# Transposing the third batch's x by DMA instead of on TensorE: pairs 8, 9 and 10 of a block-sparse attention kernel that feeds a mixture of experts

## The chip, the cores and the metric

One core of a Trainium2 chip (trn2); the rounds of the experiments ran on three such chips, each beside the kernel before. The metric is the device time of one execution in microseconds (us); most executions of a kernel agree within 0.3%.

Engine names: PE is TensorE, PEld its weight loads, DVE VectorE, ACT ScalarE, POOL GpSimd, SP SyncE. The suffix q (SPq) means the engine's instruction queue. L508 is line 508 of the kernel's file.

## The reference

Two parts. Attention over q, k, v of shape (4, 8, 768, 64): every query sees the keys less than 16 positions away and 24 block summaries of the whole sequence (maximum of k, mean of v over 32 positions). Its output, laid out as x of shape (3072, 512), feeds a mixture of 8 experts with a Sinkhorn-normalized gate:

```python
logits = x @ w_gate                      # (3072, 8)
P = np.exp(logits - logits.max())
for _ in range(8):                       # 8 rounds over ALL rows
    P /= P.sum(1, keepdims=True) + 1e-9
    P /= P.sum(0, keepdims=True) + 1e-9
    P *= N / E
for e in range(8):
    out += P[:, e:e+1] * (np.maximum(x @ w1[e], 0) @ w2[e])
```

The Sinkhorn rounds need the logits of all four batches, so they cannot start before the last batch's x is complete.

## The kernel before

Attention works in "pairs": pair i holds two heads, pairs 0 to 3 are batch 0, 4 to 7 batch 1, 8 to 11 batch 2, 12 to 15 batch 3. Each pair's normalized output `xs` must be transposed into `xT`, which expert 0, the gate's logits and all other experts read. There are two ways, both already in the kernel:

```python
def to_xT(i, h=None):                    # way 1: PE transposes into PSUM ...
    t = at.pop(("xs", i, h or 0))
    tx = at["tx", i, h] = bank("a", "tx", BF16)
    for g in range(G if h is None else HG):
        nc.tensor.transpose(tx[:, g * 128:(g + 1) * 128],
                            t[:, g, :, :].rearrange("p j d -> p (j d)"), ident)

def x_out(eng, i, h=None):               # ... and a copy by ACT or DVE into xT
    ...
    copy(eng, xT[:, i % PB, t0:t0 + n], at.pop(("tx", i, h))[:, 0:n])

def x_dma(i):                            # way 2: one DMA transpose, SBUF to SBUF
    t, t0 = at.pop(("xs", i, 0)), i // PB * S
    nc.sync.dma_start_transpose(
        out=xT[:, i % PB, t0:t0 + S].rearrange("c (g t) -> c g t", g=G),
        in_=t[:].rearrange("p g j d -> p (g j d)"))
```

The order of the instructions on every engine is static. While the kernel is built, a small planner simulates the engines with assumed durations and lists each unit where it would run. This is the planner's choice of the two ways (`lag` is time until landing):

```python
X_BY_DMA = 12
# ... at the end of pair_whole(i, prio), PB = 4:
if i >= X_BY_DMA and i % PB < PB - 1:
    U["xt", i] = add("SP", 1.5, lambda: x_dma(i), [U["no", i, 0], U["no", i, 1]], prio)
    U["x", i] = add("DMA", 1.7, None, [U["xt", i]], prio, lag=2.0)
    return
buf = Buffer("a")
U["xt", i] = add("PE", 0.35, lambda: to_xT(i), [U["no", i, 0], U["no", i, 1]], prio, opens=[buf])
U["x", i] = add({"ACT": 0.8, "DVE": 0.55}, 0, lambda: x_out(U["x", i].on, i), [U["xt", i]], prio, uses=[buf])
```

So before the change pairs 12, 13 and 14 go by DMA and all others, also the last pair of each batch, by PE. Expert 0's matmuls serve as filler for PE between attention's units. The last piece is how expert 1's weights are fetched. POOL issues two loads of 1 MB, and first reads a column of the last pair's transposed k and q, so that the loads wait for those transposes:

```python
def transposed():
    r = (NP - 1) % NB                    # NP - 1 is pair 15
    nc.gpsimd.tensor_copy(out=warm[:, 0:1], in_=kT[r][0:32, 0:1])
    nc.gpsimd.tensor_copy(out=warm[:, 1:2], in_=qT[r][0:32, W:W + 1])
    ...                                  # two more, of the near values
last[0] = add("POOL", 0.3, transposed, ...)
load("w1n", lambda: load_w1(1), 0.85, 5.0)
load("w2n", lambda: load_w2(1), 0.85, 5.0)
```

The softmax here doesn't subtract the row's maximum and nothing guards it: scores larger than these inputs give would overflow.

Of the kernel before, what the change touches and what calls it, by code (L numbers as in the profile page):

```python
# [32 lines left out]
class Plan:  # L33
# [7 lines left out]
    def add(self, eng, cost, fn, deps=(), prio=0.0, opens=(), uses=(), lag=0.0):  # L41
        u = Unit(eng, cost, fn, [d for d in deps if d is not None], prio, list(opens), lag)
        for b in list(opens) + list(uses):
            b.users.append(u)
        if uses and eng != "PE":
            u.prio -= 100.0
        self.units.append(u)
        return u
# [64 lines left out]
def kernel(  # L113
# [28 lines left out]
    VD = D + 1  # L142
    NEH = 3
    BY_DMA = 12
    X_BY_DMA = 12
    WHOLE = 12

    const = ctx.enter_context(tc.tile_pool(name="const", bufs=1))
# [71 lines left out]
    with tc.tile_pool(name="attn", bufs=1) as attn, \  # L220
# [295 lines left out]
        def x_dma(i):  # L516
# [4 lines that stand above are left out]
# [188 lines left out]
        def pair_whole(i, prio):  # L709
# [27 lines left out]
            for h in range(2):  # L737
# [5 lines left out]
                                    [U["A", i, h], U.get(("x", i - 2))], prio, uses=[buf])  # L743
            if i >= X_BY_DMA and i % PB < PB - 1:
                U["xt", i] = add("SP", 1.5, lambda: x_dma(i), [U["no", i, 0], U["no", i, 1]], prio)
# [175 lines left out]
```

## Time and profile before

| | before |
|---|---|
| time, median of 4 runs | 738.88 us (738.64 to 739.21) |
| span of the profiled execution | 740.0 us |
| PE transposes of x / DMA transposes of x | 78 / 3 |
| wait of PE at the last logits | 0.85 us |

The profiled execution itself took 741.82 us; PE's clock was halved in it from 14.2 to 21.0 us, before anything that the change touches.

The page's first part gives busy time, share of the span and number of instructions of each engine:

```profile
PE 730.5 (99%) x4300; PEld 355.8 (48%) x4300; DVE 369.2 (50%) x728; ACT 198.4 (27%) x339; POOL 95.8 (13%) x122
```

PE is busy 99% of the span. The stretch table (columns: stretch, its length, then busy time and count of PE, PEld, DVE, ACT, POOL; then PE's granted clock, 1.00 being full speed, DMA share, GB/s):

```profile
66.00:94.20 28.20, 27.36 (x314) 18.00 (x315) 26.89 (x74) 20.54 (x35) 15.68 (x22) 1.00 1.61 134
94.20:124.90 30.70, 30.50 (x293) 18.12 (x291) 20.11 (x55) 19.24 (x37) 6.48 (x14) 1.00 0.58 91
124.90:126.00 1.10, 0.25 (x7) 0.16 (x5) 0.00 (x0) 0.50 (x2) 0.00 (x0) 1.00 0.16 10
126.00:156.00 30.00, 30.00 (x189) 16.45 (x190) 23.34 (x65) 14.70 (x29) 4.46 (x1) 1.00 0.01 1
```

PE has 0.84 us free in the 28.2 us of the stretch in which the change lies, and 0.2 us in the next. The one larger hole lies after it, at 124.9 to 126.0. The timeline of PE around that hole (start, duration, engine, line, operation, output<-inputs, partitions and shapes, count; in brackets the idle time before it and what ended it):

```profile
121.94 0.50 PE L508 MATMUL tx<-ident,xs 128*128 128x128 bf16 x6
122.27 2.76 PE L206 MATMUL hps<-xT,w_347 128*128 128x384 bf16 x16
124.87 0.20 PE L528 MATMUL lp<-wg_bf,xT 128*128 128x8 bf16 x2
125.91 0.71 PE L528 MATMUL lp<-wg_bf,xT 128*128 128x8 bf16 x22 [0.85 <-DMA xT<-xs]
```

`tx` is the PE transpose of pair 15's x, `hps` are expert 0's matmuls, and `lp` are the last batch's logits. PE runs two of the logits and then waits 0.85 us for a DMA, the transpose of pair 14's x. That DMA's own view, and the timeline of POOL, which had started the weight loads 8 us before the DMA was issued:

```profile
L518 SPq DMA_TRANSPOSE xT<-xs x1: 1261/1261/1261, 118.3 to 118.3; - x1
...
DMA to landing us min/median/max: 7.6/7.6/7.6
```

```profile
109.01 0.17 POOL L834 CAST warm<-Ve_125 32x1 f32<-32x1 bf16 x1
109.99 0.18 POOL L834 CAST warm<-Ve_125 32x1 f32<-32x1 bf16 x1 [0.81 <-DMA Ve_125<-vx_112]
110.23 0.79 POOL L187 DMA_DIRECT2D w_2344<-in_moe_w_dram  x1
111.00 0.91 POOL L193 DMA_DIRECT2D w_2368<-in_moe_w_dram  x1
```

The DMA was issued at 118.26 and landed after 7.6 us.

### The profile page before, as it was taken

Reading aid. Unit: us, or ns where it says so; the run is one execution under the profiler, and the core shown is the slowest. Engines: PE = TensorE matmul, PEld = TensorE weight load, DVE = VectorE, ACT = ScalarE, POOL = GpSimd, SP = SyncE. Lnnn points to the kernel's source line nnn. Section 1 sums busy time; section 2 is a strip of 40 time slices with the busy share of each in tenths; the row PEclk is TensorE's granted clock in tenths of the full one; section 3 lists DMA queues with packets and bytes.
Section 4 is the critical chain, followed back from the end, with each engine's and each line's share of the span. In section 5 each row is a group of like instructions: output and inputs, shape, how many; then the busy total and the mean of one; then the engine's idle time right before and its main releaser. Section 6 shows DMA issues by size and latency. Waiting matters only on the chain.

```text
span 740.0 us, 10176 instructions
## 1 busy us (share of the span) xinstructions
PE 730.5 (99%) x4300; PEld 355.8 (48%) x4300; DVE 369.2 (50%) x728; ACT 198.4 (27%) x339; POOL 95.8 (13%) x122
## 2 busy tenths in 40 slices
PE   8999999999999999999999999999999999999998
PEld 4666655544444444444444444444444444444444
DVE  7789975774444444444443444444444444444443
ACT  5678665441111111111111111121121121121120
POOL 8799330040000000000000000000000000000000
PEclk8999999999999999999999999999999999999999
DMA  9999918033003300212003300222003300001213
GB/s 132 179 144 147 139 28 125 1 65 50 0 1 58 57 1 1 40 28 47 0 1 58 57 1 1 48 29 39 0 1 58 57 1 1 0 1 58 99 72 114
DMA packets 95389, 35.84 MB, mean 48 GB/s; under 512 B 76016, under 2 KB 88816, under 8 KB 95344
## 3 DMA queue, kind: packets, MB, share of 16 engines
q0 software_dynamic: 79344, 26.39, 33.1%
q1 hardware_dynamic: 15328, 8.66, 4.9%
q8 instruction: 34, 0.56, 0.3%
q10 hardware_dynamic: 672, 0.15, 0.1%
q14 instruction: 11, 0.09, 0.0%
HBM read 52.45 MB, written 6.29 MB: 79 GB/s over the span
## 4 chain that ended last, share of the span: by engine, by line
PE 89%; DVE 7%; DMA 2%; POOL 1%; issue 1%; POOLq 0%
PE hps L206 43%; PE yps L211 42%; DVE xs L501 2%; DMA xT<-xs 1%; DMA vx_110<-in_v_dram 1%; DVE em L387 1%; PE av L470 1%; PE sg L324 1%; DVE ks_104 L315 1%; DVE ks_103 L315 1%; PE ss L422 0%; DVE rc L500 0%; PE vs L332 0%; PE tx L508 0%; DVE Ve_124 L342 0%
## 5 line engine op out<-in xcount | busy, mean ns | idle before, releaser
L197 ACT ACTIVATE h<-hps 128x512 bf16<-128x512 f32 (+1 forms) x219 | 125.3, 572 | 475.1 <-PE hps L206 474.1
L211 PEld LDWEIGHTS <-h 128*128 128x128 bf16 x1544 | 150.4, 98 | 175.2
L199 DVE TENSOR_SCALAR h<-hps 128x512 bf16<-128x512 f32 (+1 forms) x181 | 123.5, 682 | 175.8 <-PE hps L206 174.5
L879 DVE SCALAR_TENSOR_TENSOR out_acc<-yps,P_sb,out_acc 128x512 f32<-128x512 f32 (+1 forms) x169 | 126.4, 748 | 165.9 <-PE yps L211 165.8
L206 PE MATMUL hps<-xT,w_347 128*128 128x384 bf16 x256 | 47.5, 326 | 0.0
L211 PE MATMUL yps<-w_501,h 128*128 128x512 bf16 x192 | 46.3, 379 | 0.0
L206 PE MATMUL hps<-xT,w_2868 128*128 128x512 bf16 x192 | 42.4, 379 | 0.0
L206 PE MATMUL hps<-xT,w_3968 128*128 128x512 bf16 x192 | 42.4, 379 | 0.0
L211 PE MATMUL yps<-w_3970,h 128*128 128x512 bf16 x192 | 42.4, 379 | 0.0
L206 PE MATMUL hps<-xT,w_5582 128*128 128x512 bf16 x192 | 42.4, 379 | 0.0
L211 PE MATMUL yps<-w_2368,h 128*128 128x512 bf16 x192 | 42.4, 379 | 0.0
L211 PE MATMUL yps<-w_2870,h 128*128 128x512 bf16 x192 | 42.4, 379 | 0.0
L206 PE MATMUL hps<-xT,w_4506 128*128 128x512 bf16 x192 | 42.4, 379 | 0.0
L211 PE MATMUL yps<-w_4508,h 128*128 128x512 bf16 x192 | 42.4, 379 | 0.0
L206 PE MATMUL hps<-xT,w_3430 128*128 128x512 bf16 x192 | 42.4, 379 | 0.0
L211 PE MATMUL yps<-w_3432,h 128*128 128x512 bf16 x192 | 42.4, 379 | 0.0
L206 PE MATMUL hps<-xT,w_5044 128*128 128x512 bf16 x192 | 42.4, 379 | 0.0
L211 PE MATMUL yps<-w_5046,h 128*128 128x512 bf16 x192 | 42.4, 379 | 0.0
L211 PE MATMUL yps<-w_5584,h 128*128 128x512 bf16 (+1 forms) x200 | 42.3, 370 | 0.0
L206 PE MATMUL hps<-xT,w_2344 128*128 128x512 bf16 x192 | 42.3, 379 | 0.0
L206 PEld LDWEIGHTS <-w_347 128*128 128x128 bf16 x256 | 23.5, 99 | 13.4
L206 PEld LDWEIGHTS <-w_3968 128*128 128x128 bf16 x192 | 18.8, 98 | 22.6
(256 smaller groups left out, 567.4 us busy)
## 6 DMA issues: line engine op xcount, KB each, us to landing
out_dram<-out_acc SPq DMA_DIRECT2D x23, 256.0 KB, 2.0
qst<-in_q_dram POOLq DMA_DIRECT2D x32, 96.0 KB, 5.6
kst<-in_k_dram POOLq DMA_DIRECT2D x24, 96.0 KB, 5.6
w_347<-in_moe_w_dram POOLq DMA_DIRECT2D x4, 256.0 KB, 7.1
w_501<-in_moe_w_dram POOLq DMA_DIRECT2D x1, 1024.0 KB, 10.5
w_2344<-in_moe_w_dram POOLq DMA_DIRECT2D x1, 1024.0 KB, 8.1
w_2368<-in_moe_w_dram POOLq DMA_DIRECT2D x1, 1024.0 KB, 14.2
w_2868<-in_moe_w_dram POOLq DMA_DIRECT2D x1, 1024.0 KB, 14.9
```

Source lines behind the costliest of these rows:

```text
L197: nc.scalar.activation(out=out, in_=in_, func=AF.Relu, bias=0.0, scale=1.0)
L199: nc.vector.tensor_scalar_max(out=out, in0=in_, scalar1=0.0)
L206: nc.tensor.matmul(hp[:, 0:n], lhsT=w1s[e][:, dk, f * 128:(f + 1) * 128], rhs=xT[:, dk, t0:t0 + n], start=(dk == 0), stop=(dk == KD - 1))
L211: nc.tensor.matmul(yp[:, d], lhsT=h[:, f, c * 128:(c + 1) * 128], rhs=w2s[e][:, f, d], start=(f == 0), stop=(f == KF - 1))
L315: nc.vector.tensor_reduce(out=ks[i % 2][:, 0, 0:24], in_=kT[r][:].rearrange("p (n w) -> p n w", w=32), axis=AX.X, op=ALU.max)
L324: nc.tensor.matmul(dst, lhsT=kT[r][p0:p0 + 64, g * 128:(g + 1) * 128], rhs=qT[r][p0:p0 + 64, g * 128 + l0:g * 128 + l1], start=True, stop= ...
L387: nc.vector.tensor_tensor(out=at["em", i][:, :, c, :], in0=at["er", i][:, :, c, W:W + 128], in1=band[:, None, None, W:W + 128].to_broadcas ...
L470: nc.tensor.matmul(av[p0:p1, o:o + n], lhsT=lhsT, rhs=rhs, start=start, stop=stop, skip_group_check=True)
L501: nc.vector.tensor_tensor(out=t.rearrange("p g j d -> p (g j) d"), in0=av[:, :, 0:D], in1=rc[:].to_broadcast([128, G, D]), op=ALU.mult)
L879: nc.vector.scalar_tensor_tensor(out=out_acc[:, t, d], in0=yp[:, d], scalar=P_sb[:, t, e:e + 1], in1=out_acc[:, t, d], op0=ALU.mult, op1=A ...
```

## The change

The intent: PE is the bottleneck, so take work off it. The third batch's pairs 8, 9 and 10 join the DMA way; 18 PE transposes and 3 copies go. The whole diff:

```diff
-    X_BY_DMA = 12
+    X_BY_DMA = 8
```

## The prediction

> **What bounds the kernel.** PE: the busy table has it at 730.5 of 740.0 us, the chain of waits is PE for 89%. After 156 us PE runs expert matmuls back to back. The change touches only the attention phase, where expert 0's matmuls fill PE's gaps: in the stretch table PE is busy 27.36 of 28.20 us from 66.0 to 94.2, and 30.50 of 30.70 from 94.2 to 124.9. DVE is nearly as full in the first stretch (26.89): it paces the attention chain there.
>
> **Removed.** The timeline shows for each of pairs 8, 9, 10 (at 72.5, 80.3, 86.2 us) six PE transposes; PE's next instruction starts 0.34 us later (80.28 to 80.62), so PE saves 3 x 0.34 = 1.0 us. (The Trainium skill, "TensorE: Matmul & The Clock Gate", Part 4, measured about 390 ns for one transpose in isolation; here, pipelined, the pitch is 56 ns.) With them go the PSUM evacuations, 0.56 (DVE), 0.80 (ACT), 0.55 us (DVE), and PE's wait of 0.24 us on DVE ahead of pair 8's transposes.
>
> **Added.** Three DMA transposes of 1.21 us each on SP's queue (tile view). SP is in order and busy between 70.8 and 89.8 us with near-value copies and the k/q transposes of pairs 12 to 15, which are delayed by 1.3 to 4 us. Landing is slow while loads run: kT_99, issued at 74.2, took 6.9 us; kT_102, issued at 87.2, took 2.7. The Trainium skill, "DMA: Bandwidth & Descriptors", section "Issuing engines are not separate DMA queues", says that all queues run on the same 16 engines and interleave; those landings agree. I expect x of pairs 8 to 10 to land 4 to 9 us after its normalization instead of about 1.3.
>
> **On the critical path.** The late landing should be hidden. Expert 0 first reads this batch's x at 108.9 us, some 15 us after it is complete now. Its logits (94.2 us) have filler around them. The normalization two pairs later, which reuses the xs buffer, comes 7 to 16 us later. The k/q transposes have slack: kT_100 lands at about 86 and is read at 90.4, kT_102 at about 90 and is read at 104.8; pair 12's scores start at 95.5. So what counts is PE work plus PE bubbles: 1.0 us less work, 0.2 us less wait. Against that: each engine's order is a static schedule from assumed durations, so removing units reshuffles it; it allows 5.2 us for an x transpose, and where one lands later an in-order engine stalls, as now at the last logits (0.85 us, for pair 14's x, which landed after 7.6 us next to 2 MB of weights). I take back 0.2 to 0.3 us for that.
>
> **Predicted: 738.0 us (-0.13%), 8 in 10 between 736.6 and 739.9.** Faster by over 2%: 0.01; within 2%: 0.97; slower by over 2%: 0.02.
>
> **What would show it.** 60 PE transposes of x instead of 78, PE busy and span each about 1.0 us lower. Six x transposes in SP's queue, the new ones landing 4 to 9 us after normalization; k/q transposes of pairs 12 to 15 issued 1 to 4 us later. No new PE wait over 0.5 us for x of pairs 8 to 10. DVE busy down 1.1, ACT 0.8 us. After 156 us everything only shifted.
>
> **What would make it wrong.** PE or DVE stalling at the third batch's logits or at a normalization because an x transpose lands late; pair 12's scores late because of its k/q transposes; the gain swallowed at the last logits if pair 14's x still lands at 125.9 us; a reshuffled order with more bubbles, or by luck fewer (then 2 us or more could be gained).

## The result, and the profile after

| | before | after |
|---|---|---|
| median, 4 runs each | 738.88 us | 739.80 us (739.09 to 740.78) |
| ratio of fast runs, 95% interval | | 1.0013 (0.9996 to 1.003) |
| PE transposes / DMA transposes of x | 78 / 3 | 60 / 6 |
| PE waits at the last logits | 0.85 us | 2.15 us |

A ratio is the mean time of one kernel's fast runs over that of the other's in the same rounds, so it is not quite the ratio of the medians. The time is the same within 2%, and if anything 0.9 us longer, where 0.9 us shorter had been predicted.

The lines that answer to those above, first the busy line:

```profile
PE 724.6 (98%) x4214; PEld 353.5 (48%) x4282; DVE 368.2 (50%) x727; ACT 197.3 (27%) x337; POOL 90.7 (12%) x122
```

PE busy fell by 5.9 us, but 86 matmul records fewer are in the trace where 18 transposes were removed, so that number is not to be believed. The weight loads of PE, as many as its matmuls (4300) in the trace before, fell by exactly 18. The stretch table of the changed kernel:

```profile
66.00:94.20 28.20, 27.40 (x324) 17.76 (x325) 26.85 (x75) 19.98 (x35) 17.34 (x25) 1.00 1.79 136
94.20:121.30 27.10, 27.00 (x249) 16.04 (x249) 17.43 (x47) 16.66 (x33) 5.80 (x12) 1.00 0.67 106
121.30:124.20 2.90, 0.75 (x25) 0.66 (x24) 0.00 (x0) 0.51 (x2) 0.00 (x0) 0.91 1.13 181
124.20:128.40 4.20, 4.20 (x26) 2.29 (x23) 1.51 (x4) 1.68 (x4) 0.00 (x0) 0.66 0.02 3
```

Attention is as full as before: no bubbles came in (0.8 us free of 28.2, 0.1 of 27.1). The hole at the last logits has grown to 2.9 us with 0.75 us of work in it, and a new thing follows: from 124.2 to 128.4 PE's granted clock is 0.66. The same on PE's timeline:

```profile
119.64 0.50 PE L508 MATMUL tx<-ident,xs 128*128 128x128 bf16 x6
119.98 1.47 PE L206 MATMUL hps<-xT,w_347 128*128 128x384 bf16 x8
121.28 0.20 PE L528 MATMUL lp<-wg_bf,xT 128*128 128x8 bf16 x2
123.63 0.74 PE L528 MATMUL lp<-wg_bf,xT 128*128 128x8 bf16 x22 [2.15 <-DMA xT<-xs]
124.22 4.16 PE L206 MATMUL hps<-xT,w_347 128*128 128x384 bf16 x16
128.22 0.28 PE L547 MATMUL sink<-csum_sb,col_en 128*128 128x8 f32 x2
```

PE waited 2.15 us for pair 14's x, and the next 16 matmuls of expert 0 took 4.16 us; before, 16 of them took 2.76. And the DMA and POOL:

```profile
L518 SPq DMA_TRANSPOSE xT<-xs x1: 1294/1294/1294, 112.3 to 112.3; - x1
...
DMA to landing us min/median/max: 11.2/11.2/11.2
```

```profile
108.29 0.58 POOL L831 CAST warm<-qT_98 32x1 f32<-32x1 bf16 x1 [3.00 <-DMA qT_98<-qst]
...
109.28 0.79 POOL L187 DMA_DIRECT2D w_2384<-in_moe_w_dram  x1
110.06 0.92 POOL L193 DMA_DIRECT2D w_2395<-in_moe_w_dram  x1
```

Pair 14's x was issued at 112.33 us and landed 11.2 us later, at 123.6.

These two profiles cannot be laid on each other by their clock times, because the start of a kernel varies: five profiles of the *same* changed kernel reach pair 7's x transposes, which come before the first changed instruction, at 65.86, 69.81, 66.31, 65.85 and 67.45 us. The latest of them had a granted clock of 0.83 and 0.66 in the two stretches from 10 to 30 us. So from here on a trace is measured from the start of pair 7's six `tx` transposes (67.98 us in the trace before, 65.86 after; the kernel before has this one trace only):

| from pair 7's transposes to ... | before | after | difference |
|---|---|---|---|
| first of the two weight loads issued | 42.25 | 43.42 | +1.17 |
| pair 14's x issued to DMA | 50.28 | 46.47 | -3.81 |
| PE reaches the last logits | 56.89 | 55.42 | -1.47 |
| pair 14's x landed | 57.9 | 57.7 | -0.2 |
| expert 1's first matmul | 88.28 | 89.54 | +1.26 |

This table is the whole story of the trace. PE does arrive 1.47 us earlier. But the x that it needs there was issued 3.8 us earlier and landed at the same moment. The gain turns into waiting: -1.47 of arrival, +1.30 of wait (2.15 - 0.85), +1.40 by the slower clock (4.16 - 2.76) make +1.23 against the measured +1.26.

### The profile page after: what moved, and what is told of

It is laid out like the page before. It is cut to its first block, busy times and chain, and to the rows that moved or that the text cites. A ratio compares the mean times of both kernels' runs of the same rounds, so it can differ in the third digit from the quotient of the medians.

```text
span 739.0 us, 10076 instructions
## 1 busy us (share of the span) xinstructions
PE 724.6 (98%) x4214; PEld 353.5 (48%) x4282; DVE 368.2 (50%) x727; ACT 197.3 (27%) x337; POOL 90.7 (12%) x122
## 4 chain that ended last, share of the span: by engine, by line
PE 90%; DVE 5%; DMA 3%; POOL 1%; issue 1%; ACT 0%; POOLq 0%
PE hps L206 43%; PE yps L211 43%; DMA xT<-xs 2%; DVE xs L501 1%; DMA vx_112<-in_v_dram 1%; PE sg L324 1%; DVE em L387 1%; DVE ks_104 L315 1%; PE av L470 1%; PE ss L422 0%; PE vs L332 0%; PE tkq L283 0%; POOL kst L258 0%; DVE rc L500 0%; DVE h L199 0%
## 5 line engine op out<-in xcount | busy, mean ns | idle before, releaser
L206 PE MATMUL hps<-xT,w_347 128*128 128x384 bf16 x256 | 49.2, 333 | 0.0
L211 PE MATMUL yps<-w_501,h 128*128 128x512 bf16 x180 | 44.4, 379 | 0.9 <-issue 0.3
L211 PE MATMUL yps<-w_4487,h 128*128 128x512 bf16 x188 | 42.2, 379 | 0.3
L211 PE MATMUL yps<-w_2395,h 128*128 128x512 bf16 x189 | 42.3, 379 | 0.2
L211 PE MATMUL yps<-w_3949,h 128*128 128x512 bf16 x189 | 42.3, 379 | 0.2
L211 PE MATMUL yps<-w_5025,h 128*128 128x512 bf16 x188 | 42.2, 379 | 0.2
L211 PE MATMUL yps<-w_2849,h 128*128 128x512 bf16 x187 | 42.2, 379 | 0.3
L211 PE MATMUL yps<-w_3411,h 128*128 128x512 bf16 x188 | 42.0, 379 | 0.2
```

Of the source, the lines that this page charges most:

```text
L206: nc.tensor.matmul(hp[:, 0:n], lhsT=w1s[e][:, dk, f * 128:(f + 1) * 128], rhs=xT[:, dk, t0:t0 + n], start=(dk == 0), stop=(dk == KD - 1))
L211: nc.tensor.matmul(yp[:, d], lhsT=h[:, f, c * 128:(c + 1) * 128], rhs=w2s[e][:, f, d], start=(f == 0), stop=(f == KF - 1))
```

## The experiments

**Theory A.** The change saves its PE time, and loses it at the last logits, because pair 14's x lands with the weight loads and not when it is issued. The clock drop follows from the longer idle gap.
**Theory B** (rival). The change costs time where it acts: three more transposes in SP's in-order queue delay k and q, the static order is reshuffled, and late x transposes stall DVE.

### c1: the changed kernel again

> The changed kernel, unaltered, as control in the same rounds. Theory A (PE gains 1.2 to 1.4 us in the attention phase and loses it at the last logits, waiting about 2.15 us instead of 0.85 for pair 14's x, which lands only when the 2 MB of weights beside it have landed; in some executions PE's clock drops after that gap and costs up to 1.3 us more): 739.1 to 740.8 us, runs with a clock of 1.0 at the lower end, runs with 0.997 to 0.998 at the upper end; the wait at the last logits again 1.8 to 2.5 us. Theory B (the loss is inside the attention phase: three more transposes in SP's in-order queue delay the k/q transposes and the reshuffled order has more bubbles): the same time, but PE not ahead of the kernel before when it reaches the last logits.

739.55 us median (738.66 to 743.38, 6 runs), ratio 1.0014 (0.9993 to 1.0035). The wait at the last logits was 2.24 us, pair 14's x landed after 11.3 us. PE reached the logits 55.42 us after pair 7, as in the first trace and 1.47 earlier than before. There was no clock drop in this trace, and expert 1 started after 88.20 us: 0.08 less than before, although this run was the slowest of the six (743.38 us; it lost its time before 30 us). That is theory A's sum without the drop, -1.47 + 1.39 = -0.08. The early arrival in both traces speaks against theory B.

### c2: pair 14 back on PE

```diff
-            if i >= X_BY_DMA and i % PB < PB - 1:
+            if i >= X_BY_DMA and i % PB < PB - 1 and i != 14:
```

> The changed kernel, but pair 14's x goes by PE transposes again (the DMA transposes of pairs 8, 9, 10, 12, 13 stay). Theory A: no DMA transpose left beside the weights, so the 2.15 us wait and the clock drop go, 0.34 us of PE transposes come back: 737.3 to 738.2 us, ratio to the kernel before 0.998 to 0.999, clock 1.0 in every run. Theory B: the SP queue is nearly as full in 70 to 95 us, so no gain: 739.3 or more. Risk to both: the static order moves.

738.52 us median, but spread from 736.63 to 740.98 over 6 runs; ratio 0.9996 (0.9975 to 1.0017). The median missed the forecast, as did "clock 1.0 in every run" (two had 0.993 and 0.995), and the times alone decide nothing. PE's order also changed a little with this edit. In the trace the wait and the drop are gone, and pair 7 to expert 1 took 86.08 us, 2.2 less than before the change; the traced run was the fastest of the six.

### c3 and c4: the weight loads after pair 14's x, with and without the change

The same edit on the changed kernel (c3) and on the kernel before (c4). POOL reads a column of pair 14's x before it issues the loads:

```diff
+            nc.gpsimd.tensor_copy(out=warm[:, 4:5], in_=xT[0:32, 2, 3 * S:3 * S + 1])
 ...
-        last[0] = add("POOL", 0.3, transposed, [last[0], U["near", NP - 1]] + ...)
+        last[0] = add("POOL", 0.3, transposed, [last[0], U["near", NP - 1], U["x", NP - 2]] + ...)
```

> The changed kernel; GpSimd reads one column of pair 14's x before it issues the two weight loads, so those start only when that x has landed. The order of the instructions on PE, DVE, ACT and SP is the same as in the changed kernel. Theory A: pair 14's x lands about 3 us after its issue instead of 11.2, PE waits 0 to 0.3 us at the last logits, no clock drop: 737.0 to 737.8 us, ratio 0.998. Theory B: the order is unchanged, so the time stays at 739.3 or more.

> The same edit on the kernel before (order elsewhere the same). Theory A: its 0.85 us wait at the last logits goes: 738.0 to 738.3 us; the changed kernel with the same edit is then faster by 0.7 to 1.3 us, which is what the change is worth with the weights out of the way. Theory B: also about 738.1 us, and the changed kernel with the edit not faster than it.

c3: 737.39 us median (736.57 to 739.08), ratio 0.9976 (0.9961 to 0.9991): faster than the kernel before, though by far less than 2%. Its order on PE, DVE, ACT and SP is that of the changed kernel, checked instruction by instruction; only the start of two loads moved. Pair 14's x landed after 2.7 us and PE did not wait at the logits. A reshuffled order as theory B's cause is thereby refuted: the same order, without the loads beside that one DMA, is faster.

c4: 738.82 us median (737.89 to 741.15), ratio 1.0 (0.9982 to 1.0019). The forecast was 738.0 to 738.3 and was missed; two of its six runs had a clock of 0.995. The expectation was also wrong in saying that the order stays: in c4 the planner moved the logits two groups of expert 0's matmuls forward on PE. Its trace shows no wait, and 87.20 us from pair 7 to expert 1.

Between c4 and c3, with the loads out of the way in both, the change is worth 738.82 - 737.39 = 1.4 us by the medians, or 1.0 us without c4's two runs at 0.995 (738.40). By the two traces it is only 87.20 - 87.02 = 0.18 us, because c3's has the wait described next; against d1 below, whose trace has no such wait, it is 87.20 - 85.83 = 1.37 us. (c4's logits stand a little earlier, so it differs from the others in more than the change.)

c3's trace shows that theory B has a small part of the truth. The waits of DVE in it, from 64 to 100 us (what waited, for what: us in total, times, longest):

```profile
DVE xs L501 <- DMA xT<-xs: 1.3, 1, 1.3
```

Pair 9's x was issued at 79.6 us, among the attention loads, and landed after 9.6 us, and a normalization that reuses its buffer stood 1.3 us. In the other traces of this order it landed sooner: none in the first trace, in c1 and d1, 0.4 us in one later look. With that wait, pair 7 to expert 1 took 87.02 us in c3.

### d1: only the second load late

```diff
         load("w1n", lambda: load_w1(1), 0.85, 5.0)
+        last[0] = add("POOL", 0.2, lambda: nc.gpsimd.tensor_copy(out=warm[:, 4:5], in_=xT[0:32, 2, 3 * S:3 * S + 1]),
+                      [last[0], U["x", NP - 2]])
         load("w2n", lambda: load_w2(1), 0.85, 5.0)
```

> The changed kernel, but only the second of the two weight loads (1 MB) waits until pair 14's x has landed; the first stays where it was. The order on PE, DVE, ACT and SP is the same as in the changed kernel. Theory A (x of pair 14 lands when the loads queued ahead of it have landed): it lands with the first load, 5 to 6.5 us after its issue (11.2 in the changed kernel, 2.7 with both loads late), which is before PE reaches the last logits, 9 us after that issue: no wait there; 737 to 738 us. Theory B: as the changed kernel, 739.3 us or more.

737.05 us median (736.56 to 737.92), ratio 0.9971 (0.9958 to 0.9985): the lowest median, though not to be told from c3's in other rounds, and faster than the kernel before. Again the order on PE, DVE, ACT and SP is the changed kernel's. With one load beside it, pair 14's x lands after 6.0 us:

```profile
L518 SPq DMA_TRANSPOSE xT<-xs x1: 1249/1249/1249, 112.2 to 112.2; - x1
...
DMA to landing us min/median/max: 6.0/6.0/6.0
```

```profile
121.17 0.74 PE L528 MATMUL lp<-wg_bf,xT 128*128 128x8 bf16 x24
121.77 2.76 PE L206 MATMUL hps<-xT,w 128*128 128x384 bf16 x16
```

PE reaches the logits 55.45 us after pair 7, as in the changed kernel (55.42), so the gain arises at the logits: no wait there, and the 16 matmuls take 2.76 us. Pair 7 to expert 1: 85.83 us, 2.45 less than before the change. The same DMA at the same point of the program thus landed after 2.7 us with no load beside it, 6.0 with one, and 11.2 to 11.8 with two. With two it lands 5.5 to 5.9 us after the first load and 1.3 to 1.4 us before the second, so c1's wording, that it lands only when both have landed, is a little too strong.

### d2: the wait filled with idle matmuls

```diff
-            lp = at["lp", b] = bank("a", "lp")[:, 0:G * E]
+            bk = bank("a", "lp")
+            if b == B - 1:
+                for _ in range(10):
+                    nc.tensor.matmul(bk[:], lhsT=zeros[:, 0:128], rhs=zeros[:], start=True, stop=True)
+            lp = at["lp", b] = bk[:, 0:G * E]
```

> The changed kernel with ten idle matmuls (about 2.16 us) on PE just ahead of the last logits, in place of its idle wait; everything else in the same order. The wait is still paid, only not idle. If the clock drop after the wait (clock 0.50 from 124 to 127 us in the changed kernel's first trace, absent in its second) is caused by the idle gap: time between 738.7 and 739.4 us, no run with a clock of 0.997 to 0.998 and 740 to 741 us other than by the start of the kernel; time from the last logits to expert 1's first matmul the same as in the kernel before. If the removal of the wait itself were not what helped in the kernels with late loads, this one would gain as much as they did (737.4).

740.18 us median (739.24 to 742.85), ratio 1.0021 (1.0002 to 1.0039). The forecast of at most 739.4 was missed, and one run had 742.85 us at a clock of 1.0, so the timed runs do not show what the idle gap costs. They do show that keeping PE busy through the wait brings none of the gain that removing the wait brought. In the trace: no drop, 88.40 us from pair 7 to expert 1, which is the kernel before (88.28) again. The traced run was the fastest of the six (739.24 us); why the others took up to 742.85 us is not shown.

### d3: the logits later in PE's order, the loads where they were

```diff
-                U["x", i] = add("DMA", 1.7, None, [U["xt", i]], prio, lag=2.0)
+                U["x", i] = add("DMA", 1.7, None, [U["xt", i]], prio, lag=2.0 if i < NP - 2 else 9.0)
```

> The changed kernel with the schedule told that pair 14's x takes 7 us longer, so that it puts expert 0's matmuls ahead of the last logits; the loads stay where they were and the x lands as late as before. Theory A: PE's wait at the last logits goes or shrinks below 0.5 us, and time falls to 737.0 to 738.0 us as with the late loads. Theory B: 739.3 or more. Risk: the normalization rounds after the logits move 2 to 3 us later on DVE and eat into their slack before expert 1.

738.09 us median (736.35 to 740.68, three of six runs with a clock of 0.995 to 0.998), ratio 0.9987 (0.9967 to 1.0007); just outside the forecast and unclear by times. In the trace pair 14's x still landed after 11.3 us, but PE had expert 0's work until then and waited for nothing:

```profile
122.39 4.06 PE L206 MATMUL hps<-xT,w 128*128 128x384 bf16 x24
...
127.15 0.74 PE L528 MATMUL lp<-wg_bf,xT 128*128 128x8 bf16 x24
```

Pair 7 to expert 1 took 85.74 us, although this trace, like the one before the change, lost time at the start (clock 0.73 from 10 to 20 us). In this trace, then, the late landing itself was harmless; what costs is to reach the place that needs it too early.

### d4: also pairs 4, 5 and 6 by DMA, loads late

```diff
-    X_BY_DMA = 8
+    X_BY_DMA = 4
```

> The changed kernel with both loads late, and x of pairs 4, 5, 6 by DMA too (six more... three pairs more: another 54 - 36 = 18 PE transposes less). Theory A: again about 1.0 to 1.4 us of PE time less, 736.0 to 736.8 us, if those x land in time; but they are issued at 45 to 65 us, where DMA is fully busy and near-value copies fill SP's queue, so DVE may stall at normalizations two pairs later as it did once for 1.25 us in the kernel with both loads late. If it stalls at each, the gain is gone: 737.4 or more.

This kernel has c3's edit besides. 742.2 us median (740.41 to 744.34), ratio 1.0044 (1.0024 to 1.0063): slower. The optimistic branch of the forecast failed. It is not the normalizations that stall but the transposes of k and q and the near values, which share SP's queue. PE's waits from 40 to 135 us in its trace, and DVE's on a DMA (`av` is attention times values, `ss` the scores against the summaries, `tkq` a transpose of k or q):

```profile
PE av L416 <- DMA Ve<-vx: 2.0, 2, 1.5
PE ss L422 <- DMA qT<-qst: 1.8, 1, 1.8
PE tkq L283 <- ACT xT L202: 0.7, 1, 0.7
```

```profile
DVE ks L315 <- DMA kT<-kst: 1.9, 1, 1.9
```

PE was busy only 25.07 of the 28.20 us from 66.0 to 94.2. Theory B is what happens here, at twice the dose; at the dose of the change it was not.

### e1 to e4: how often does the clock drop?

Four single profiles, three of the changed kernel and one of d2's.

> The changed kernel, one more profile, to see how often PE's clock drops after the gap at the last logits (it did in the first trace, 0.50 from 124 to 127 us, not in the second). If every gap of over 2 us had a chance of about a half, one or two of these three looks show it, each time at a cost of 1.3 to 1.4 us between the last logits and expert 1's first matmul; a look without it takes the same time from pair 7's transposes to expert 1 as the kernel before (88.2 us).

> The changed kernel, the second of three more profiles: one or two of the three show the drop of the clock after the gap at the last logits, the others 88.2 us from pair 7's transposes to expert 1.

> The changed kernel, the third of three more profiles: one or two of the three show the drop of the clock after the gap at the last logits, the others 88.2 us from pair 7's transposes to expert 1.

> The kernel with the wait filled by idle matmuls, one more profile: no drop of the clock between 120 and 130 us, 88.2 to 88.5 us from pair 7's transposes to expert 1's first matmul. A drop here would show that the gap is not its cause.

All three looks at the changed kernel show the drop, more than expected, and at a higher cost (1.4 to 2.5 us). e4 shows none, as expected, and 88.54 us, just outside the forecast. Their single times (741.89, 742.47, 743.23 us; state unknown) are those of profiled executions and are not compared. The longest drop, on PE's timeline of e2, and the filled wait of e4:

```profile
121.27 0.19 PE L528 MATMUL lp<-wg_bf,xT 128*128 128x8 bf16 x2
123.99 0.75 PE L528 MATMUL lp<-wg_bf,xT 128*128 128x8 bf16 x22 [2.53 <-DMA xT<-xs]
124.60 5.28 PE L206 MATMUL hps<-xT,w 128*128 128x384 bf16 x16
```

```profile
123.84 2.32 PE L527 MATMUL lp<-zeros 128*128 128x512 bf16 x10
126.00 0.19 PE L532 MATMUL lp<-wg_bf,xT 128*128 128x8 bf16 x2
126.61 0.70 PE L532 MATMUL lp<-wg_bf,xT 128*128 128x8 bf16 x22 [0.42 <-DMA xT<-xs]
127.18 2.76 PE L206 MATMUL hps<-xT,w 128*128 128x384 bf16 x16
```

In e2 the 16 matmuls after the gap took 5.28 us; in e4, after a wait filled with idle matmuls up to the last 0.42 us, 2.76. All traces together:

| trace | idle wait at the last logits | 16 matmuls after it | pair 7 to expert 1 |
|---|---|---|---|
| before | 0.85 | 2.76 | 88.28 |
| after | 2.15 | 4.16 | 89.54 |
| c1 | 2.24 | 2.76 | 88.20 |
| e1 | 2.73 | 4.16 | 90.19 |
| e2 | 2.53 | 5.28 | 91.23 |
| e3 | 2.26 | 4.44 | 90.38 |
| d2 (filled) | 0.26 | 2.76 | 88.40 |
| e4 (filled) | 0.42 | 2.76 | 88.54 |
| d1 | none | 2.76 | 85.83 |

Four of five gaps of 2.15 to 2.73 us were followed by a drop that cost 1.4 to 2.5 us in these 16 matmuls; neither of the two filled waits was.

Why c1's gap was not: in the packed traces every drop between the kernel's start and its last instructions lasts 3.41 us or twice that, and its edges lie on steps of 3.41 us counted from the first clock mark. In the four traces with a drop, 2.0 to 2.7 us of the gap lie within one such step (after 2.15, e1 2.73, e2 2.01, e3 2.26), and the drop begins at the end of that step. In c1 an edge splits the gap into 1.45 and 0.79 us. This fits the five traces, but it is not shown to be the rule: before 30 us a drop also followed a step with only 1.1 us idle (c1), while a step with 1.3 us idle (c2) had none after it.

How often it happens in other runs can be narrowed, because every timed run lists its mean granted clock. A drop of 3.41 us to half speed takes 0.0023 off the mean of a 739 us run (an estimate from these figures), so a run listed at 0.999 or 1.0 had none. Of the changed kernel's ten timed runs (four in the result, six in c1) the two traced ones are listed at 0.997 and 0.993, two at 0.998, and six at 0.999 or 1.0: at most two of the eight untraced runs had the drop. The median of those six is 739.16 us, against 738.88 for the kernel before at such clocks in c1's rounds. Without the drop the change is thus worth about nothing (+0.3 us, within the scatter), as in c1's trace (-0.08).

## Why the prediction was right or wrong

The range and the class (within 2%) held, the range by luck more than by the argument: 739.80 us lies 0.1 us inside its upper end, and two of the four runs lie outside. The direction did not hold: -0.9 us was predicted and +0.9 us measured, within an interval that includes no change.

- *"PE saves 3 x 0.34 = 1.0 us", "0.2 us less wait"*: right, even a little low. PE reaches the last logits 1.47 us earlier in three traces of the changed kernel (55.42 against 56.89 us), and 1.38 and 0.97 us earlier in e1 and e3. The 0.24 us wait that was to go did not: it moved to the matmul that took the transposes' place. But three other short waits went (0.34, 0.23 and 0.20 us) and two of 0.16 us came, which with the 1.0 us makes 1.45.
- *"The late landing should be hidden"*: right for pairs 8 to 10. They landed 6.7, 7.8 and 6.5 us after issue, and no wait on them is in the trace after; c3 shows that the slack is thin (one wait of 1.3 us).
- *k/q transposes "delayed by 1.3 to 4 us"*: wrong for the later ones. Counted from pair 7's transposes, pair 12's k is 1.9 us later, but the q of pair 15 is 18.9 us later (20.6 to 39.5 us), because the planner put x of pairs 12 and 13 in front of it. This was harmless for attention, but the weight loads wait for that q. They start 1.17 us later against the rest of the program. No run moved them back by that, so how much of the longer wait at the logits comes from it is not known.
- **The step that failed:** *"I take back 0.2 to 0.3 us for that."* This was the term for in-order engines that stall where an x lands late. The sum treated the 0.85 us wait at the last logits as a constant of the kernel and gave the new stalls 0.2 to 0.3 us. But that wait ends when pair 14's x lands, and beside the two loads that hardly moved (57.9 and 57.7 us), although the x was issued 3.81 us earlier. So what PE saved ahead of it was waited there: the wait grew by 1.30 to 1.88 us. In four of five traces the clock drop, which the prediction did not have at all, added 1.4 to 2.5 us. The prediction named this among what would make it wrong (*"the gain swallowed at the last logits if pair 14's x still lands at 125.9 us"*) and did not put it into the sum.

The cause is shown, not only argued: with the order of all compute engines unchanged, moving one load of 1 MB (d1) turned a ratio of 1.0014 (c1) into 0.9971 (in other rounds and on another chip, each against the kernel before); leaving the loads and moving the logits (d3) gave the same 85.7 to 85.8 us in the trace.

Open: how much of the +0.9 us is due to the clock drop (the four runs took 740.78 and 739.98 us at 0.997 and 0.998, 739.62 and 739.09 at 1.0); whether the idle gap alone causes it, which rests on four of five gaps against none of two filled waits; and why single runs of d2 and c2 took 741 to 743 us at a clock of 1.0.

## What to carry to other kernels

Before counting work saved on the busiest engine as time, look for the next point on that engine which waits for something whose time does not depend on it, here a DMA behind a large load: work saved ahead of such a point becomes waiting, and work saved behind it is gained. When a transfer becomes urgent, look at what else is issued in the few microseconds before it; a load that is needed 40 us later can start after it. If the saving cannot be seen in the total, measure distances between two instructions that both traces have, since the start of the kernel alone scattered by 4 us here.

## What the Trainium skill lacked or had wrong

- "TensorE: Matmul & The Clock Gate", Part 1 and "Why this matters for your kernels", says that the clock falls to half after an idle window of about 3.4 us and warns of gaps over about 3 us. Here waits of 2.15, 2.26, 2.53 and 2.73 us were already followed by a granted clock of 0.50 (one of 2.24 us was not); that waits of 0.85 (before), 1.24 (c3) and 1.81 us (d4) were not agrees. A window need not be idle throughout: 2.0 to 2.7 us within one step of 3.41 us were enough. The page's free-running window fits why the same gap drops the clock in one execution and not in the next: c1's gap lay across two steps (see e1 to e4).
- "DMA: Bandwidth & Descriptors", section "Queues, rings and completion order", says that each DMA engine takes turns between its queues by packet, but gives no time for a small transfer beside large loads. Here a DMA transpose of 192 KB landed after 2.7 us alone, 6.0 beside one load of 1 MB, and 11.2 to 11.8 beside two that had been issued 2 to 3 us ahead of it. It landed 5.5 to 5.9 us after the first of them and 1.3 to 1.4 us before the second.
- "TensorE: Matmul & The Clock Gate", Part 4, gives about 390 ns (275 in a kernel) for one PE transpose and no figure for a row of them. Six in a row cost PE 0.34 us here, 56 ns each, which is the pitch that Part 1 gives for matmuls of that size; between other matmuls it is the pitch that counts.
